# An attention and gated-MLP kernel on one core: fewer zero-weight matmuls, ten exponential buffers, other constants in the planner

## The chip, the cores and the metric

The kernel runs on one core of a Trainium2 chip. The metric is the device time of one execution in microseconds. The kernel before took 746.0 us (median of three runs, 745.09 to 746.49). The profile shown here is of one more execution, which took 744.99 us, with a span of 743.1 us from its first to its last instruction.

Five engines work side by side, each on its own queue of instructions: TensorE (PE: matmuls; PEld: its weight loads), VectorE (DVE), ScalarE (ACT), GpSimd (POOL) and SyncE (SP, here only DMA issues). They wait for one another by semaphores.

## The reference

```python
xn = layernorm(x)                          # x: 1 x 2048 x 512
q = (xn @ wq) as 32 heads of 16; k = xn @ wk; v = xn @ wv     # one k and v for all heads
p = softmax(q @ k.T * 16**-0.5)            # 2048 x 2048 for each of 32 heads
s = (p @ v, heads side by side) @ wo
h = silu(xn @ w_gate) * (xn @ w_up)        # 512 -> 1792
g = silu(h @ w_down)
out = x + s * g
```

The bulk is the exponential of 32 x 2048 x 2048 scores.

## The kernel before

Scores are made transposed, 128 keys by 512 queries of one head in a matmul that uses 32 rows of the array. Two heads fill one *score tile* of 128 x 1024 in PSUM (`sc_emit`, L890). There are 1024 score tiles, in 32 blocks (4 query chunks x 4 groups of 8 heads x 2 halves), 32 tiles to a block. Three PSUM rings of 1024 columns hold them: rings 0 and 1 serve ScalarE, ring 2 serves VectorE.

The exponential of a tile is taken on one of two engines:

- ScalarE: one `ACTIVATE Exp` from ring 0 or 1 into a bf16 buffer `Pb` (`act_sc`, L950). The first few of block 1 go into the space of `g2_sb` instead (8 tiles).
- VectorE: a bit trick in two passes. `passA` (L1004) turns a tile of ring 2 into integers whose bits read as fp16; two tiles make a *pair*, and two shifted copies (`dS`, L1020) are added, so that three approximations with different errors are summed by the matmuls.

The products with V (`pv_emit`, L760) accumulate in the one bank `o_ps`. They use 32 columns of the array for each head, so four matmuls (a *column group*) run side by side. A pair of ScalarE tiles costs one column group with `VA`, a VectorE pair three with `VD`. At the end of a block VectorE moves `o_ps` out (`oev`, L773). Between these TensorE also does the MLP, the Q projections and the output projection as *fill* column groups into `m_ps` (`cmm`, L491); ScalarE does 72 `Tanh` for the two silus, 56 for the gate (L666) and 16 after the down projection (L686).

All of this is interleaved by a planner that runs while the program is built. `_Sched` gives each operation an engine, a planned duration and its dependencies, and places it at the earliest planned time; `pe_pick` chooses what TensorE does next. Then everything is emitted in planned order, and each engine's queue is chained in that order. Planned times therefore decide only the order; on the chip the semaphores decide when.

Names that the change touches:

- `MMF` is the planned duration of a column group or of a score tile, `SWITCH` the planned cost of going from score matmuls (row strips) to column groups or back.
- `TOL`: a column group may go ahead of the next ScalarE score tile if it ends at most `TOL` after the time at which that tile could start.
- `NPB` is the number of `Pb` buffers. The exponential of tile k writes buffer k mod `NPB`, and waits for the column group that read the tile `NPB` earlier (`pb_rel`).
- `PB_URG`: as long as fewer than that many ScalarE tiles are outstanding (their column group is not yet placed), column groups of the current block rank behind fill; from there on they rank first.
- `ACTMIN`: where nothing is ready for TensorE for at least one column group and a switch, `pe_pick` puts a group of four matmuls with zero weights there (`zw`), which adds nothing to the open sum in `o_ps` or `m_ps`. It does so only if `activity`, the planned TensorE work that started in the last 1.8 us (a score tile counts 0.107 us, transposes and the small V projections nothing), is under `ACTMIN`. With 9.0 that is always so.

The lines that decide it:

```python
if Tz - F >= MMF + sd.switch("c") and (act_ < ACTMIN or cur["issued"] == NTILE):
    ...
            return F, ("zero", bb)
...
ex = OP("ACT", 0.904, [sc, pb_rel[k - NPB] if k >= NPB else None, cur["exp"]], emit, (1,), name="exp")
...
if ts is None or tm + sd.switch(co.mode) + co.dur <= ts + TOL:
    cands.append(tm)
```

Of the kernel before, what the change touches and what calls it, by code (L numbers as in the profile page):

```python
# [32 lines left out]
NWARM, NJUNK = 13, 200  # L33
D_START, D_LIM, D_LIM_END = 26, 12, 8
F_ON, F_OFF = 26, 60
PB_URG, AHEAD, LAZY, ACTMIN, ACTLOW = 6, 16, 8, 9.0, 0.8
DPRI, DTOL, DWIN = -1.0, 0.12, 0.15
TOL, MERGE = 0.17, 0.25


def _dims(A_x, A_wq, B_w_gate):
# [143 lines left out]
class _Sched:  # L185
    LAT = {"PE": 0.205, "ACT": 0.22, "DVE": 0.25, "POOL": 0.16, "DMA": 0.0, "EXT": 0.0}
    SAME = {"PE": 0.0, "ACT": 0.0, "DVE": 0.1, "POOL": 0.05, "DMA": 0.0}
    SWITCH = 0.105
    HOT = 0.3
    LOCKS = ("dS", "xn")  # L190

# [40 lines left out]
    def switch(self, mode):  # L232
        return self.SWITCH if self.mode is not None and mode != self.mode else 0.0

# [51 lines left out]
def kernel(  # L286
# [13 lines left out]
    nc = tc.nc  # L300
# [72 lines left out]
    xn = [sb([P, D], BF16, f"xn{i}") for i in range(4)]  # L373
    res = xn
    QB = [sb([P, 512], BF16, f"QB{i}") for i in range(2)]
    NPB = 8
    Pb = [sb([P, 1024], BF16, f"Pb{i}") for i in range(NPB)]
    XB = [g2_sb[:, 2 * i:2 * i + 2, :].rearrange("p n d -> p (n d)") for i in range(NT // 2)]
    Bf = [sb([P, 2048], U16, f"Bf{i}")[:] for i in range(6)]
# [117 lines left out]
    def OP(eng, dur, deps, emit, prio, mode=None, name=""):  # L497
        return sd.new(_Op(eng, dur, deps, emit, prio, mode, name))
# [3 lines left out]
        o.start = o.end = t  # L502
        return o

    MMF = 0.215
    NBLK = NSC * NQ * 2
    LN = 4 * (NSC - 1)
    NTILE = NBLK * NT * 2
# [144 lines left out]
    def hT_use(sc, f):  # L653
        return [hT_rd[0][1]] if hT_rd[0] is not None and hT_rd[0][0] == sc - 1 else []
    hT_last = [None]

    def g_ffn(sc, f):
# [3 lines left out]
        def mm(w, kc):  # L661
# [3 lines left out]
        s_ = OP("DVE", 0.6, [a, ab_rel[i]], lambda: nc.vector.tensor_copy(out=ab[i][:], in_=m_ps[:]), (1,), name="gev")  # L665
# [4 lines left out]
        u_ = OP("DVE", 0.6, [t_, b], lambda: nc.vector.scalar_tensor_tensor(  # L670
            out=th[i][:], in0=th[i][:], scalar=1.0, in1=m_ps[:], op0=ALU.add, op1=ALU.mult), (1,), name="umul")
        m_rel[:] = [u_]
        h = OP("POOL", 1.25, [u_, s_] + hT_use(sc, f), lambda: nc.gpsimd.tensor_tensor(  # L673
            out=hT[:, f, :], in0=ab[i][:], in1=th[i][:], op=ALU.mult), (0,), name="hmul")
        ab_rel[i] = th_rel[i] = h
        h_done[f] = h
# [256 lines left out]
    def act_sc(i, b, x, start, dur=MMF):  # L933
# [7 lines left out]
        else:  # L941
            cur["ba"] = b
            k = cur["nA"]
            cur["nA"] += 1
            buf = Pb[k % NPB][:]
            pb_rel.append(None)
        if k >= NPB:
            assert pb_rel[k - NPB] is not None
        def emit():
            bi = nc.scalar.activation(out=buf, in_=ring[i][:], func=ACT.Exp, scale=escale, bias=ebias)  # L950
            if k >= NPB:
                tc.declare_no_dep(bi.ins, exp_ins[k - NPB].ins,
# [457 lines left out]
```

## Time and profile before

| | |
|---|---|
| median of three runs | 746.0 us |
| the profiled execution | 744.99 us, span 743.1 us |
| mean granted TensorE clock | 0.996 |
| busy: TensorE, ScalarE, VectorE, GpSimd | 721.5, 718.1, 682.4, 127.0 us |
| ScalarE exponentials | 736, of 1181 ns each (728 into `Pb`, 8 of 1148 ns into `g2_sb`) |
| score tiles on VectorE | 288 (144 pairs), `passA` 1219 ns |

Busy time of a group of instructions is the union of their intervals. Consecutive ScalarE instructions overlap in the trace (one starts before the other has ended), so the step from start to start, not the duration, is what one costs. The ends of matmuls are modelled. "Idle before" is the time in which an engine had nothing in flight, with what ended it. A DMA is not the limit anywhere after the first 40 us: the mean over the span is 28 GB/s.

### The profile page before, as it was taken

What the parts mean: (1) busy time and instruction counts of PE and PEld (TensorE: products, weight loads), DVE (VectorE), ACT (ScalarE), POOL (GpSimd) and SP (SyncE); (2) the same over time, 40 slices, a digit from 0 to 9 for tenths busy, and PEclk for the clock granted to TensorE, in tenths of its full rate; (3) what the DMA queues carried; (4) which work ended last, traced back from release to release, by engine and by line L of the source; (5) the groups of instructions that cost most, each with busy time, mean ns of one, the idle gap of its engine ahead of it and who ended that gap; (6) DMA issues with size and microseconds to landing.
All of it is one profiled execution on the core that took longest, in us unless ns stands there. A gap on an engine that the chain in (4) does not pass through costs nothing.

```text
span 743.1 us, 20569 instructions
## 1 busy us (share of the span) xinstructions
PE 721.5 (97%) x8999; PEld 217.0 (29%) x8999; DVE 682.4 (92%) x886; ACT 718.1 (97%) x822; POOL 127.0 (17%) x120
## 2 busy tenths in 40 slices
PE   8999999999999999999999999999999999999994
PEld 3332222222222222222222322222222322322231
DVE  7779999999999899999999999999989999999995
ACT  5999999999999999999999999999999999999992
POOL 3212222200022222200013121220003222220001
PEclk9999999999999999999999999999999999999998
DMA  9400000000011100000001000000001000000001
GB/s 326 151 24 3 23 3 23 2 11 17 3 30 38 38 3 8 18 2 24 3 25 45 21 19 3 25 2 9 17 2 31 24 23 3 6 20 2 24 30 34
DMA packets 21722, 20.68 MB, mean 28 GB/s; under 512 B 8760, under 2 KB 17720, under 8 KB 21624
## 3 DMA queue, kind: packets, MB, share of 16 engines
q1 hardware_dynamic: 20040, 18.73, 8.3%
q8 instruction: 72, 1.18, 0.7%
q10 hardware_dynamic: 1584, 0.56, 0.3%
q14 instruction: 26, 0.21, 0.1%
HBM read 14.71 MB, written 2.34 MB: 23 GB/s over the span
## 4 chain that ended last, share of the span: by engine, by line
ACT 59%; PE 34%; DVE 4%; issue 2%; POOL 0%; ACTq 0%; DVEq 0%; POOLq 0%
ACT Pb L950 54%; PE ring L890 12%; PE o_ps L760 12%; PE m_ps L491 9%; ACT th L666 3%; ACT g_sb L950 1%; DVE Bf L1020 1%; DVE Bf L1004 1%; ACT th L686 1%; DVE x_sb L1020 1%; DVE x_sb L1004 1%; PE ring L491 0%; DVE ab L665 0%; PE ring L455 0%; DVE xn L708 0%
## 5 line engine op out<-in xcount | busy, mean ns | idle before, releaser
L950 ACT ACTIVATE Pb<-ring 128x1024 bf16<-128x1024 f32 x728 | 687.9, 1181 | 3.8 <-PE ring L890 1.9
L890 PE MATMUL ring<-QB,KT 32*128 32x512 bf16 x2048 | 291.7, 383 | 7.1 <-ACT Pb L950 3.9
L1004 DVE TENSOR_SCALAR Bf<-ring 128x1024 uint16<-128x1024 f32 x172 | 209.7, 1219 | 10.9 <-PE ring L890 9.2
L890 PEld LDWEIGHTS <-KT 32*128 32x128 bf16 x2048 | 84.9, 91 | 301.2 <-issue 297.1
L1004 DVE TENSOR_SCALAR x_sb<-ring 128x1024 uint16<-128x1024 f32 x116 | 141.5, 1220 | 7.6 <-PE ring L890 5.8
L760 PE MATMUL o_ps<-Pb,VA 128*32 128x512 bf16 x1456 | 140.5, 385 | 0.0
L673 POOL TENSOR_TENSOR hT<-ab,th 128x512 bf16<-128x512 f32 x56 | 78.2, 1396 | 356.7 <-DVE th L670 356.7
L760 PE MATMUL o_ps<-Bf,VD 128*32 128x512 f16 x1044 | 95.1, 384 | 1.2 <-DVE Bf L1020 1.1
L491 PE MATMUL m_ps<-wd_sb,hT 128*32 128x512 bf16 x896 | 72.5, 382 | 0.0
L491 PE MATMUL m_ps<-xnT,wg_sb 128*32 128x512 bf16 x896 | 72.3, 383 | 0.1
L1020 DVE TENSOR_SCALAR Bf<-Bf 128x2048 uint16<-128x2048 uint16 x101 | 72.1, 723 | 0.2
L491 PE MATMUL m_ps<-xnT,wu_sb 128*32 128x512 bf16 x896 | 68.4, 382 | 0.0
L760 PE MATMUL o_ps<-x_sb,VD 128*32 128x512 f16 x684 | 64.1, 384 | 0.0
L760 PEld LDWEIGHTS <-VD 128*32 128x32 f16 x1728 | 38.4, 94 | 60.1 <-issue 50.5
L760 PEld LDWEIGHTS <-VA 128*32 128x32 bf16 x1472 | 36.8, 94 | 54.2 <-issue 50.6
L1020 DVE TENSOR_SCALAR Bf<-x_sb 128x2048 uint16<-128x2048 uint16 x74 | 50.8, 694 | 0.3
L1020 DVE TENSOR_SCALAR x_sb<-Bf 128x2048 uint16<-128x2048 uint16 x71 | 50.5, 716 | 0.4
L745 POOL TENSOR_TENSOR oT<-oa,rb 128x512 bf16<-128x512 f32 x15 | 19.7, 1313 | 162.8 <-DMA rb<-dscr 153.0
L665 DVE COPY ab<-m_ps 128x512 f32<-128x512 f32 x56 | 38.3, 685 | 6.8 <-PE m_ps L491 6.4
L666 ACT ACTIVATE th<-ab 128x512 f32<-128x512 f32 x56 | 43.7, 781 | 0.0
L670 DVE SCALAR_TENSOR_TENSOR th<-th,m_ps 128x512 f32<-128x512 f32 x56 | 38.2, 682 | 4.0 <-PE m_ps L491 3.4
L1020 DVE TENSOR_SCALAR x_sb<-x_sb 128x2048 uint16<-128x2048 uint16 x42 | 29.5, 703 | 0.1
(115 smaller groups left out, 332.8 us busy)
## 6 DMA issues: line engine op xcount, KB each, us to landing
rb<-dscr SPq DMA_DIRECT2D x15, 256.0 KB
out_dram<-xn SPq DMA_DIRECT2D x16, 128.0 KB, 1.9
dn<-oa SPq DMA_DIRECT2D x120, 2.0 KB, 1.7
oa<-oa SPq DMA_DIRECT2D x60, 32.0 KB, 2.0
wg_sb<-in_B_w_gate_dram SPq DMA_DIRECT2D x1, 1792.0 KB, 11.6
wu_sb<-in_B_w_up_dram SPq DMA_DIRECT2D x1, 1792.0 KB
wd_sb<-in_B_w_down_dram SPq DMA_DIRECT2D x1, 1792.0 KB, 20.5
x_sb<-in_A_x_dram SPq DMA_DIRECT2D x3, 512.0 KB
```

Of the source, the lines that this page charges most:

```text
L491: return [nc.tensor.matmul(out=dst[GRP * j:GRP * j + GRP, :], lhsT=w[:, GRP * j:GRP * j + GRP], rhs=rhs, start=start, stop=stop, tile_posi ...
L665: s_ = OP("DVE", 0.6, [a, ab_rel[i]], lambda: nc.vector.tensor_copy(out=ab[i][:], in_=m_ps[:]), (1,), name="gev")
L666: t_ = OP("ACT", 0.477, [s_, th_rel[i]], lambda: nc.scalar.activation(out=th[i][:], in_=ab[i][:], func=ACT.Tanh, scale=0.5), (0,), name="t ...
L670: u_ = OP("DVE", 0.6, [t_, b], lambda: nc.vector.scalar_tensor_tensor(out=th[i][:], in0=th[i][:], scalar=1.0, in1=m_ps[:], op0=ALU.add, op ...
L673: h = OP("POOL", 1.25, [u_, s_] + hT_use(sc, f), lambda: nc.gpsimd.tensor_tensor(out=hT[:, f, :], in0=ab[i][:], in1=th[i][:], op=ALU.mult) ...
L686: t_ = OP("ACT", 0.477, [a, th_rel[i]], lambda: nc.scalar.activation(out=th[i][:, :D], in_=m_ps[:, :D], func=ACT.Tanh, scale=0.25), (0,), ...
L745: return [pk, q], lambda eng: eng.tensor_tensor(out=oT[qs % 2][:, jj, :], in0=o0[:], in1=rbt[:], op=ALU.mult)
L760: r.append(nc.tensor.matmul(out=o_ps[GRP * g:GRP * g + GRP, :], lhsT=lhs, rhs=rhs, start=(n == 0), stop=(n == pv_total[(b, g)] - 1), tile_ ...
L890: return lambda: [nc.tensor.matmul(out=ring[sl][:, u * 512:(u + 1) * 512], lhsT=KT[half][GRP * g:GRP * g + GRP, t * P:(t + 1) * P], rhs=QB ...
L950: bi = nc.scalar.activation(out=buf, in_=ring[i][:], func=ACT.Exp, scale=escale, bias=ebias)
L1004: lambda: nc.vector.tensor_scalar(out=U[:, hs], in0=ring[si][:], scalar1=ubias, scalar2=UINF, op0=ALU.add, op1=ALU.min), (1.5, u), name="p ...
L1020: o = OP("DVE", 0.6, [pa, pa0] + wrel, lambda wi=wi, i=i: nc.vector.tensor_scalar(out=Bf[wi], in0=U, scalar1=SHIFT[i], scalar2=None, op0=A ...
```

## The change

Nothing in the kernel's arithmetic changes, only constants: those of the planner, the count of `Pb` buffers, and the planned duration of one GpSimd operation.

```diff
-PB_URG, AHEAD, LAZY, ACTMIN, ACTLOW = 6, 16, 8, 9.0, 0.8
+PB_URG, AHEAD, LAZY, ACTMIN, ACTLOW = 9, 16, 8, 0.6, 0.8
-TOL, MERGE = 0.17, 0.25
+TOL, MERGE = 0.21, 0.25
-    SWITCH = 0.105
+    SWITCH = 0.11
-    NPB = 8
+    NPB = 10
-    MMF = 0.215
+    MMF = 0.216
-        h = OP("POOL", 1.25, [u_, s_] + hT_use(sc, f), lambda: nc.gpsimd.tensor_tensor(
+        h = OP("POOL", 1.3, [u_, s_] + hT_use(sc, f), lambda: nc.gpsimd.tensor_tensor(
```

Counted over the whole program, the order of instructions changes as follows.

| | before | now |
|---|---|---|
| zero-weight column groups into `o_ps` / into ring 2 | 84 / 1 | 17 / 0 |
| ScalarE exponentials | 736 | 738 |
| VectorE tiles (`passA`) | 288 | 286 |
| column groups with `VA` / `VD` | 368 / 432 | 369 / 429 |
| fill column groups | 808 | 808 |
| steps from one ScalarE score tile to the next with no or one column group between (fill and zero groups count, transposes and V projections do not) | 63 | 94 |
| the same with two | 477 | 466 |
| the same with three or more | 195 | 177 |

TensorE early in the program, around the fourth and fifth ScalarE score tile (`ring0`, `ring1`; `zw` are the zero weights, `KT` the keys, `VA` the values). Before (each row stands for its two or four strips, weight loads left out):

```order
L890 MATMUL ring1_97<-QB0_118,KT0_84 128x512
L760 MATMUL o_ps_99<-Pb0_120,VA_86 32x512
L760 MATMUL o_ps_99<-Pb1_121,VA_86 32x512
L760 MATMUL o_ps_99<-xnT_81,zw_149 32x512
L890 MATMUL ring0_96<-QB0_118,KT0_84 128x512
```

Now, the same place and a little on:

```order
L890 MATMUL ring1_97<-QB0_118,KT0_84 128x512
L760 MATMUL o_ps_99<-Pb0_120,VA_86 32x512
L760 MATMUL o_ps_99<-Pb1_121,VA_86 32x512
L890 MATMUL ring0_96<-QB0_118,KT0_84 128x512
L1259 MATMUL ring2_98<-x_sb_101,ident_bf_61 128x512
```

The zero group after the column group is gone, and the next score tile follows directly; behind it one plain matmul with the identity stands where before two zero groups stood.

TensorE at the last of the four V projections (L472, 16 small matmuls), before. The rows lie between the 32nd and the 33rd ScalarE score tile:

```order
L890 MATMUL ring1_97<-QB0_118,KT0_84 128x512
L491 MATMUL m_ps_100<-xnT_81,hT_107 32x512
L472 MATMUL ring2_98<-wv_sb_103,xnT_81 128x16
L760 MATMUL o_ps_99<-Pb4_124,VA_86 32x512
L760 MATMUL o_ps_99<-Pb6_126,VA_86 32x512
L890 MATMUL ring0_96<-QB0_118,KT0_84 128x512
```

Now, between the 30th and the 32nd:

```order
L890 MATMUL ring1_97<-QB0_118,KT0_84 128x512
L472 MATMUL ring2_98<-wv_sb_103,xnT_81 128x16
L890 MATMUL ring0_96<-QB0_118,KT0_84 128x512
L760 MATMUL o_ps_99<-Pb6_126,VA_86 32x512
L760 MATMUL o_ps_99<-Pb8_128,VA_86 32x512
L890 MATMUL ring1_97<-QB0_118,KT0_84 128x512
```

Before, two fill groups, the projection and two column groups with `VA` stood between two score tiles; now the projection stands alone, and the two column groups come after the next score tile.

TensorE around the 521st ScalarE score tile, before. Its exponential writes `Pb0`, and the column group that reads `Pb0`'s older content (with `Pb1`'s) is the last row:

```order
L890 MATMUL ring0_96<-QB1_119,KT0_84 128x512
L760 MATMUL o_ps_99<-Bf4_132,VD_109 32x512
L760 MATMUL o_ps_99<-x_sb_101,VD_109 32x512
L890 MATMUL ring1_97<-QB1_119,KT0_84 128x512
L890 MATMUL ring2_98<-QB1_119,KT0_84 128x512
L760 MATMUL o_ps_99<-Pb1_121,VA_86 32x512
L760 MATMUL o_ps_99<-Pb0_120,VA_86 32x512
```

Now the one place where a reader of a `Pb` buffer still stands behind the score tile whose exponential overwrites it is the 729th (the second row from below; its exponential writes `Pb0`):

```order
L890 MATMUL ring1_97<-QB1_119,KT1_85 128x512
L890 MATMUL ring2_98<-QB1_119,KT1_85 128x512
L760 MATMUL o_ps_99<-Bf1_131,VD_109 32x512
L760 MATMUL o_ps_99<-Bf0_130,VD_109 32x512
L890 MATMUL ring0_96<-QB1_119,KT1_85 128x512
L760 MATMUL o_ps_99<-Pb0_120,VA_86 32x512
```

Before, the reader stands two column groups and two score tiles behind (the 521st and the 681st tile alike; the 49th has it one score tile and its VectorE tile behind); now it stands directly behind.

## Rows read from the trace of the kernel before

**Rows 1.** The page, part 1: busy us, share of span, instructions.
```profile
PE 721.5 (97%) x8999; PEld 217.0 (29%) x8999; DVE 682.4 (92%) x886; ACT 718.1 (97%) x822; POOL 127.0 (17%) x120
```

**Rows 2.** Busy us by engine (PE, PEld, DVE, ACT, POOL); clock, DMA share, GB/s.
```profile
100.00:150.00 50.00, 49.25 (x616) 14.83 (x616) 47.48 (x60) 50.00 (x59) 10.95 (x8) 1.00 0.04 10
```

**Rows 3.** ScalarE in order of time: start, length, merged instructions.
```profile
300.37 6.61 ACT L950 ACTIVATE Pb<-ring 128x1024 bf16<-128x1024 f32 x7
306.70 0.78 ACT L666 ACTIVATE th<-ab 128x512 f32<-128x512 f32 x1
307.22 5.76 ACT L950 ACTIVATE Pb<-ring 128x1024 bf16<-128x1024 f32 x6
```

**Rows 4.** Line 950: count, least, median, longest ns, first and last start.
```profile
L950 ACT ACTIVATE Pb<-ring x728: 1006/1187/1355, 12.9 to 727.3; 128x1024 bf16<-128x1024 f32 x182
```

**Rows 5.** TensorE in order of time, an ordinary stretch.
```profile
303.68 0.40 PE L760 MATMUL o_ps<-Bf,VD 128*32 128x512 f16 x4
303.90 0.60 PE L491 MATMUL m_ps<-xnT,wg_sb 128*32 128x512 bf16 x8
304.44 0.39 PE L890 MATMUL ring<-QB,KT 32*128 32x512 bf16 x2
304.76 0.61 PE L491 MATMUL m_ps<-xnT,wg_sb 128*32 128x512 bf16 x8
305.31 0.40 PE L890 MATMUL ring<-QB,KT 32*128 32x512 bf16 x4
```

**Rows 6.** All zero-weight matmuls, by line: count, busy us, mean ns.
```profile
L760 PE MATMUL o_ps<-xnT,zw 128*32 128x512 bf16 x336 | 27.6, 383 | 0.0
```

**Rows 7.** ScalarE in order of time, around its three longest waits.
```profile
38.43 3.88 ACT L950 ACTIVATE Pb<-ring 128x1024 bf16<-128x1024 f32 x4
43.12 2.85 ACT L950 ACTIVATE Pb<-ring 128x1024 bf16<-128x1024 f32 x3 [0.81 <-PE ring L890]
...
507.58 10.36 ACT L950 ACTIVATE Pb<-ring 128x1024 bf16<-128x1024 f32 x11
518.83 1.94 ACT L950 ACTIVATE Pb<-ring 128x1024 bf16<-128x1024 f32 x2 [0.89 <-PE o_ps L760]
...
675.07 1.94 ACT L950 ACTIVATE Pb<-ring 128x1024 bf16<-128x1024 f32 x2 [0.89 <-PE o_ps L760]
```

**Rows 8.** TensorE in order of time, the same waits.
```profile
40.56 0.39 PE L890 MATMUL ring<-QB,KT 32*128 32x512 bf16 x2
...
41.43 0.56 PE L472 MATMUL ring<-wv_sb,xnT 128*128 128x16 bf16 x16
41.91 0.84 PE L760 MATMUL o_ps<-Pb,VA 128*32 128x512 bf16 x8
42.69 0.61 PE L890 MATMUL ring<-QB,KT 32*128 32x512 bf16 x6
...
518.38 0.83 PE L760 MATMUL o_ps<-Pb,VA 128*32 128x512 bf16 x12
```

**Rows 9.** Waits, all engines: us in total, times, longest.
```profile
DVE Bf L1004 <- PE ring L890: 9.2, 26, 0.8
...
PE o_ps L760 <- DVE Bf L1020: 1.1, 4, 0.4
```

**Rows 10.** The end: VectorE's last move of `o_ps`, TensorE's next weight load.
```profile
728.95 0.76 DVE L773 COPY oa<-o_ps 128x256 f32<-128x256 f32 x2 [1.54 <-PE o_ps L760]
...
729.92 0.20 PEld L1050 LDWEIGHTS ring<-ident_f,oa 128*128 128x128 f32 x2 [0.42 <-DVE oa L773]
```

**Rows 11.** Stretches at the end; columns as in Rows 2 (PEclk: granted clock).
```profile
734.00:736.00 2.00, 0.00 (x0) 0.00 (x0) 1.97 (x5) 0.00 (x0) 1.96 (x2) 1.00 0.21 68
736.00:738.00 2.00, 0.00 (x0) 0.00 (x0) 0.88 (x1) 0.00 (x0) 0.33 (x1) 0.70 0.41 124
```

**Rows 12.** One early stretch, instructions on `zw` alone: PE, PEld, DVE, clock.
```profile
23.00:26.00 3.00, 0.00 (x0) 0.00 (x0) 0.00 (x0) 1.00 1.08 340
```

**Rows 13.** The same stretch, instructions on `xn` alone (PE: transposes).
```profile
23.00:26.00 3.00, 0.74 (x8) 0.53 (x8) 1.11 (x4) 0.00 (x0) 1.00 1.08 340
```

## Prediction

> **What bounds the kernel now.** I began with the busy times. Two engines share the top: TensorE with 721.5 us and ScalarE with 718.1 us of a span of 743.1 us, both 97% [rows 1]. The reader is to see that the two figures do not mean the same. In the stretch from 100 to 150 us ScalarE has an instruction in flight for all of the 50 us [rows 2], so the next look is whether it really runs without a pause. In the order of time, seven exponentials start at 300.37 and the next instruction starts at 306.70: 6.33 / 7 = 0.904 us for each, though each lasts about 1.19 us [rows 3, 4]. A `Tanh` takes from 306.70 to 307.22, 0.52 us. So ScalarE's floor is a sum of steps: 735 steps of 0.904 us between the first and the last exponential (736 of them, 728 on line 950 into `Pb` and 8 into `g2_sb`), 664.4 us, and 72 `Tanh` at 0.52 us, 37.4 us; 701.8 us together. The first starts at 12.9 and the last at 727.3 [rows 4]: 714.4 us. ScalarE is late by 714.4 - 701.8 = 12.6 us in all, and short waits hide behind the overlap: six exponentials from 307.22 to 312.70 take 5.48 us where 5.42 would do [rows 3].
>
> So ScalarE is the bound, and what can be won is at most these 12.6 us, plus what a smaller number of exponentials would save. TensorE's 97% holds zero-weight matmuls for 27.6 us [rows 6], so it is not full of work; but it is in order, and what stands in front of a score tile can make ScalarE wait. From the trace, a score tile to the first column group takes 304.44 to 304.76 = 0.32 us, the next column group 0.22 us (303.68 to 303.90), two groups and the way back 0.55 us (304.76 to 305.31) [rows 5]. With two column groups between, a step takes 0.87 us, under 0.904; with three it takes 1.09 us, and ScalarE's lead shrinks by 0.18 us.
>
> **The change part by part.**
>
> *Exponentials.* There are two more on ScalarE (738): 2 x 0.904 = +1.81 us, all of it on the path, since ScalarE is the bound. VectorE has two tiles less. That is off the path: VectorE waited 9.2 us for score tiles at line 1004 alone [rows 9].
>
> *Ten buffers and `PB_URG` 9.* Before, the exponential of tiles 521 and 681 waits for a column group that stands behind two other column groups and two further score tiles on TensorE. The eleven exponentials from 507.58 last 10.36 us, so the last starts at 507.58 + 10.36 - 1.19 = 516.75 and the next could start at 517.65; it starts at 518.83, after the column groups that began at 518.38 [rows 7, 8]. That is 1.18 us. The wait at 675.07 shows the same 0.89 us of visible idle time, so I price it alike: 2 x 1.18 = -2.36 us. Now the order has one such place, tile 729, with the reader directly behind the tile. Its cost is 0 if ScalarE has its usual lead; otherwise the step to a column group, 0.32 us; at worst a whole wait as above, 1.18 us. I take the 0.32, since the distance is the shortest possible. Sum -2.04 us. Behind a waiting exponential stand all later exponentials and `Tanh`, and behind them the rings; nothing else can fill ScalarE.
>
> *The V projection.* At 43.12 ScalarE starts after four exponentials that began at 38.43 and lasted 3.88 us: due at 38.43 + 3.88 - 1.19 + 0.90 = 42.02, it was 1.10 us late [rows 7]. TensorE shows why: from the score tile at 40.56 to the one at 42.69 there are 2.13 us, with two fill groups, the 16 small matmuls (41.43 to 41.91, 0.48 us) and two column groups [rows 8]. Now only the 16 matmuls stand there: 0.32 + 0.48 + 0.33 for the way back = 1.13 us, 0.23 us over a step. Gain 1.10 - 0.23 = -0.87 us. If other transposes crowd that place it is 0; at best 1.10.
>
> *The zero groups themselves.* 67 of 84 are gone, and one into ring 2: 68 x 0.22 = 15 us of TensorE. By the plan each stood in a gap; on the chip only those cost something whose gap was not there. What this, `TOL`, `MMF` and `SWITCH` do together I read from the order: steps with three or more column groups fall from 195 to 177. 72 of them are paid for by a `Tanh` (0.52 us more room), which leaves 123 and 105. Of the 12.6 us the three long waits are 2.36 + 1.10, so 9.1 us are short ones, 9.1 / 123 = 0.074 us for each crowded step. 18 fewer: -1.3 us. The bounds: all of the short waits go (-9.1), or the wider `TOL` (0.04 us more) and `SWITCH` (0.005) are paid in full in each of the 105 steps (+4.7). I take -1.3 because the count of crowded steps is what the order shows; the 0.045 us is a permission, and whether it is used is not seen.
>
> *VectorE's shifts.* Four column groups waited for line 1020, 1.1 us of TensorE in all [rows 9]. The planned VectorE times have not changed, so I leave this at 0, with -1.1 to +1.1.
>
> *GpSimd's 1.25 to 1.3 and the end.* The operation itself is the same, and GpSimd is busy for 127 us of 743 [rows 1]: 0. In the last stretch the first transpose of the last block waits for VectorE's move of `o_ps` (728.95 + 0.76 = 729.71, weight load at 729.92 [rows 10]), not for the fill groups before it, of which there are two fewer now: 0, at best -0.4.
>
> Sum: 1.81 - 2.04 - 0.87 - 1.3 = -2.4 us. The profiled execution took 744.99 us (1.9 us around its span of 743.1) and would take 742.6. It lies 1.0 us under the median of the runs, 746.0; from the median the forecast is 743.6 us.
>
> **The clock.** The zero groups also keep TensorE's array at work, and taking them out could cost the clock. In the trace the granted clock is 1.00 (2.4 GHz) until the matmuls end at about 734; it is still 1.00 in 734 to 736, with no matmul, and falls to 0.70 on average in 736 to 738 [rows 11]. From 23 to 26 us, without one zero matmul and with eight transposes among the score tiles, it stayed 1.00 [rows 12, 13].
> The Trainium skill says otherwise of transposes (TensorE: Matmul & The Clock Gate, "Part 4: PE-mode transpose"): a transpose does not count as work for the clock the way other matmuls do. By that rule the early stretch, where transposes now stand with fewer zero groups around them, is the one that could slow. The trace of before does not contradict it, since score tiles and V projections stood between the transposes; no stretch here holds transposes alone.
>
> **The rivals.**
>
> *TensorE is the bound.* Its 97% speaks for it, its zero matmuls against. If its 15 us of removed groups came off, ScalarE's floor would stop it: all 12.6 us of lateness gone, 1.81 added, about 746.0 - 10.8 = 735; a half of it 740.
>
> *Nothing to see.* The two more exponentials and the new wait at tile 729 eat the gain, and the short waits stay: 1.81 - 2.36 + 1.18 - 0.87 = -0.2, so 745.8. For it: the removed zero groups stood in planned gaps. Against it: the two long waits have no place left in the order.
>
> *Slower: the wider tolerance.* Place: the crowded steps. `TOL` lets a third column group go ahead although the score tile could start 0.21 us earlier. If half of the 0.045 us is paid in all 177 steps, 4 us, and the -1.3 does not come: 1.81 - 2.04 - 0.87 + 4 = +2.9, so 749. It decides from 1.1 us on (1.81 - 2.04 - 0.87 = -1.1), which is 0.006 us for each of the 177 steps. Against it: 94 steps now have no or one column group (63 before), and each of those gives the lead back.
>
> *Slower: the clock falls early.* Place: score tiles 4 to 31. At 1.2 GHz a step with two groups takes 1.74 instead of 0.87 us, with three 2.2 us, 0.84 and 1.3 us over a step of ScalarE. There are about seven such steps: +6 us, 749.6. Against it: [rows 12].
>
> **How the numbers follow.** A difference under 0.2% (1.5 us) cannot be told from none. The forecast, a gain of 1.5 to 5 us, 741 to 744.5, has 0.50. TensorE as the bound, 735 to 741, has 0.08. Nothing to see, 744.5 to 747.5, has 0.27. The tolerance, 747.5 to 751, has 0.10; the clock 0.05. Faster: 0.50 + 0.08 = 0.58; same 0.27; slower 0.15. The likeliest case's own range is 741 to 744.5; eight times in ten needs the case of no change and half of the last steps on either side: 739 to 747.5.
>
> **What would show it.** Right: no exponential waits 0.9 us for `o_ps` at the ends of blocks; ScalarE steps of 0.904 us still dominate; last start minus first start near 712 us, with 737 steps and 72 `Tanh` as its floor (703.7), so lateness near 8.5 us; one wait of some 0.3 us near tile 729; at the V projection a wait of 0.2 us instead of 1.1; the granted clock at 1.00 up to the end of the matmuls. Wrong: lateness above 11 us, from many steps of 0.93 to 1.0 us (tolerance); a clock under 1.00 between 15 and 45 us; or TensorE waiting at line 760 for line 1020 more than 2 us, which would mean that VectorE's planned times, which I left alone, now decide.

## The result and the profile after

The changed kernel takes 750.77 us (median of eight runs, 748.2 to 764.18) against 745.73 us before (eight runs, 745.09 to 746.6): a ratio of 1.0063, interval 1.0045 to 1.0081. It is slower, outside the predicted range. The profiled execution took 752.13 us, with a span of 750.3 us and a mean granted clock of 0.979 (0.996 before); over all eight runs it lies between 0.955 and 0.991. Runs that lie more than 1.5% above the fastest of their kernel, as the 764.18 here, are left out of every ratio and kept in the medians, and the profiles of f1 and e6 below are of such runs.

The first look is at the page of the changed kernel: busy times, and the granted clock in 40 slices of 18.8 us each.

```profile
PE 716.2 (95%) x8720; PEld 213.9 (29%) x8720; DVE 677.1 (90%) x882; ACT 721.6 (96%) x824; POOL 127.0 (17%) x120
...
PEclk9999999999999999999999999999999999999757
...
L950 ACT ACTIVATE Pb<-ring 128x1024 bf16<-128x1024 f32 x730 | 691.6, 1172 | 6.7 <-PE ring L890 5.0
```

TensorE is busy for 5.3 us less than before [rows 1], and the kernel is longer all the same. The row that differs is the clock's: 7 and 5 tenths in two of the last three slices.

I then took ScalarE's floor apart as in the prediction, at 0.904 us after an exponential, 0.52 after a `Tanh` of the gate and 0.477 after one of the 16 others; lateness is what the steps take beyond that (13.2 us before by this count, where the prediction took 0.52 for all `Tanh` and had 12.6).

| profiled execution, us | before | after | difference |
|---|---|---|---|
| first exponential starts | 12.87 | 13.87 | +1.00 |
| floor (736 and 738 exponentials) | 701.2 | 703.0 | +1.81 |
| lateness before 700 us | 12.87 | 11.63 | -1.24 |
| lateness after 700 us | 0.35 | 6.80 | +6.45 |
| last exponential's start to the end | 15.83 | 15.05 | -0.78 |
| span | 743.1 | 750.3 | +7.2 |

The loss lies after 700 us, in the last 32 exponentials. ScalarE there, in order of time:

```profile
698.67 11.43 ACT L950 ACTIVATE Pb<-ring 128x1024 bf16<-128x1024 f32 x12
710.32 4.85 ACT L950 ACTIVATE Pb<-ring 128x1024 bf16<-128x1024 f32 x5 [0.22 <-PE ring L890]
...
719.12 1.02 ACT L950 ACTIVATE Pb<-ring 128x1024 bf16<-128x1024 f32 x1 [0.47 <-PE ring L890]
720.63 1.02 ACT L950 ACTIVATE Pb<-ring 128x1024 bf16<-128x1024 f32 x1 [0.49 <-PE ring L890]
722.14 1.02 ACT L950 ACTIVATE Pb<-ring 128x1024 bf16<-128x1024 f32 x1 [0.49 <-PE ring L890]
...
725.72 1.02 ACT L950 ACTIVATE Pb<-ring 128x1024 bf16<-128x1024 f32 x1 [1.04 <-PE o_ps L760]
```

From 719.12 on, a step takes 1.51 us (720.63 - 719.12) instead of 0.904, and each of them waits for a score tile. What TensorE did before, in order of time:

```profile
702.92 0.40 PE L760 MATMUL o_ps<-Pb,VA 128*32 128x512 bf16 x4
703.50 0.40 PE L890 MATMUL ring<-QB,KT 32*128 32x512 bf16 x4 [0.17 <-ACT Pb L950]
704.41 0.39 PE L890 MATMUL ring<-QB,KT 32*128 32x512 bf16 x2 [0.52 <-ACT Pb L950]
704.73 0.62 PE L760 MATMUL o_ps<-Pb,VA 128*32 128x512 bf16 x4
705.33 0.61 PE L890 MATMUL ring<-QB,KT 32*128 32x512 bf16 x4
```

The same column group takes 0.40 us at 702.92 and 0.62 at 704.73. Nothing late stood before it: TensorE waited 0.17 and 0.52 us for ScalarE to free a ring. The stretches of the changed kernel (columns as in [rows 2]):

```profile
695.00:700.00 5.00, 5.00 (x68) 1.27 (x60) 4.90 (x8) 5.00 (x7) 0.00 (x0) 1.00 0.16 32
702.00:704.00 2.00, 1.51 (x18) 0.58 (x15) 1.96 (x4) 2.00 (x3) 0.51 (x1) 1.00 0.19 64
704.00:706.00 2.00, 1.59 (x14) 0.47 (x13) 1.79 (x2) 2.00 (x4) 1.04 (x1) 0.68 0.00 0
706.00:708.00 2.00, 2.00 (x14) 0.34 (x11) 1.82 (x2) 2.00 (x3) 0.00 (x0) 0.50 0.00 0
720.00:724.00 4.00, 4.00 (x36) 0.70 (x32) 2.13 (x3) 2.53 (x4) 0.00 (x0) 0.50 0.02 4
728.00:732.00 4.00, 4.00 (x52) 0.92 (x44) 3.12 (x5) 3.22 (x5) 0.00 (x0) 0.92 0.00 0
```

and of the kernel before, at the same time:

```profile
704.00:708.00 4.00, 4.00 (x50) 1.19 (x48) 3.52 (x5) 4.00 (x6) 0.00 (x0) 1.00 0.02 6
```

The clock falls from 1.00 (2.4 GHz) to 0.50 (1.2 GHz) at about 704.7 us and is back at full at 728.6. Before the fall TensorE was busy for 1.51 of 2 us, never idle longer than 0.52; before the change it was busy throughout at this time. Idle time of that size does not tell a fall by itself. The kernel before has two such waits in a row at about 315 us, and its clock stays at 1.00:

```profile
314.45 0.39 PE L890 MATMUL ring<-QB,KT 32*128 32x512 bf16 x2 [0.32 <-ACT Pb L950]
315.37 0.40 PE L890 MATMUL ring<-QB,KT 32*128 32x512 bf16 x4 [0.53 <-ACT Pb L950]
```

Which part of the sparse work decides is not read from these rows. In the trace of the changed kernel the MLP's fill ends at 686.4 us, some 45 ScalarE tiles before the end (718.6 us and 10 tiles before the change), and from 700.8 to 717 us 15 of the 17 steps from one ScalarE score tile to the next hold one column group or none. Zero groups would have filled them, but the planner counts too much activity to put them there (e3 below allows them, and 31 stand in the last 50 tiles).

### The profile page after: what moved, and what is told of

Same layout as the page of the kernel before. It is cut to its first block, busy times and chain, and to the rows that moved or that the text cites. A ratio compares the mean times of both kernels' runs of the same rounds, so it can differ in the third digit from the quotient of the medians.

```text
span 750.3 us, 20016 instructions
## 1 busy us (share of the span) xinstructions
PE 716.2 (95%) x8720; PEld 213.9 (29%) x8720; DVE 677.1 (90%) x882; ACT 721.6 (96%) x824; POOL 127.0 (17%) x120
## 4 chain that ended last, share of the span: by engine, by line
ACT 55%; PE 35%; DVE 5%; issue 2%; DMA 1%; POOL 1%; SPq 0%; DVEq 0%; POOLq 0%; ACTq 0%
ACT Pb L950 51%; PE ring L890 12%; PE o_ps L760 11%; PE m_ps L491 10%; ACT th L666 3%; DVE Bf L1004 1%; ACT g_sb L950 1%; DVE Bf L1020 1%; DVE x_sb L1004 1%; ACT th L686 1%; DMA rb<-dscr 1%; DMA dscr<-rc 0%; DMA dn<-oa 0%; SPq L787 0%; DVE x_sb L1020 0%
## 5 line engine op out<-in xcount | busy, mean ns | idle before, releaser
L890 PE MATMUL ring<-QB,KT 32*128 32x512 bf16 x2048 | 297.1, 388 | 16.4 <-ACT Pb L950 13.6
L1004 DVE TENSOR_SCALAR Bf<-ring 128x1024 uint16<-128x1024 f32 x176 | 214.7, 1220 | 14.5 <-PE ring L890 12.9
L1004 DVE TENSOR_SCALAR x_sb<-ring 128x1024 uint16<-128x1024 f32 x110 | 134.1, 1219 | 7.3 <-PE ring L890 5.4
L760 PE MATMUL o_ps<-Pb,VA 128*32 128x512 bf16 x1460 | 136.4, 389 | 0.0
L491 PE MATMUL m_ps<-xnT,wu_sb 128*32 128x512 bf16 x896 | 70.5, 383 | 0.1
L1020 DVE TENSOR_SCALAR Bf<-Bf 128x2048 uint16<-128x2048 uint16 x98 | 67.5, 696 | 0.3
L760 PEld LDWEIGHTS <-VD 128*32 128x32 f16 x1716 | 40.5, 95 | 56.2 <-issue 44.6
L1020 DVE TENSOR_SCALAR x_sb<-Bf 128x2048 uint16<-128x2048 uint16 x78 | 54.8, 708 | 0.3
L773 DVE COPY oa<-o_ps 128x512 f32<-128x512 f32 (+1 forms) x33 | 22.1, 672 | 8.6 <-PE o_ps L760 8.2
## 6 DMA issues: line engine op xcount, KB each, us to landing
wg_sb<-in_B_w_gate_dram SPq DMA_DIRECT2D x1, 1792.0 KB, 11.4
```

Source lines behind the costliest of these rows:

```text
L491: return [nc.tensor.matmul(out=dst[GRP * j:GRP * j + GRP, :], lhsT=w[:, GRP * j:GRP * j + GRP], rhs=rhs, start=start, stop=stop, tile_posi ...
L760: r.append(nc.tensor.matmul(out=o_ps[GRP * g:GRP * g + GRP, :], lhsT=lhs, rhs=rhs, start=(n == 0), stop=(n == pv_total[(b, g)] - 1), tile_ ...
L773: oev[b] = sd.new(_Op("DVE", 0.6, [], lambda: [nc.vector.tensor_copy(out=oat[:, a:z], in_=o_ps[:, a:z]) for a, z in cuts], (0.2,), name="o ...
L890: return lambda: [nc.tensor.matmul(out=ring[sl][:, u * 512:(u + 1) * 512], lhsT=KT[half][GRP * g:GRP * g + GRP, t * P:(t + 1) * P], rhs=QB ...
L1004: lambda: nc.vector.tensor_scalar(out=U[:, hs], in0=ring[si][:], scalar1=ubias, scalar2=UINF, op0=ALU.add, op1=ALU.min), (1.5, u), name="p ...
L1020: o = OP("DVE", 0.6, [pa, pa0] + wrel, lambda wi=wi, i=i: nc.vector.tensor_scalar(out=Bf[wi], in0=U, scalar1=SHIFT[i], scalar2=None, op0=A ...
```

## The experiments

Theory A, formed from these rows: the clock's fall at the end costs most of the loss, and it needs two edits together, one that ends the fill early and one that takes the zero groups out of the hole. Theory B: the sparse order itself costs the time, and the clock only shows it. Lateness below is read from one profiled execution each, as in the table above; "line 734" is VectorE's idle time before the reciprocal of the denominators, in us. The times are medians. Each ratio is to runs of the kernel before on the same chip, whose medians were 745.68 to 746.21.

| kernel | tiles on ScalarE, zero groups | us, ratio to before (interval) | lateness to 700 us, after | line 734 |
|---|---|---|---|---|
| before | 736, 85 | 745.73 | 12.9, 0.4 | 1.8 |
| after | 738, 17 | 750.77, 1.0063 (1.0045 to 1.0081) | 11.6, 6.8 | 3.2 |
| e1 | 736, 75 | 747.68, 1.0023 (1.0014 to 1.0032) | 15.9, 0.9 | 4.1 |
| e2 | 738, 11 | 748.9, 1.0041 (1.0026 to 1.0056) | 15.6, 0.7 | 4.5 |
| e3 | 740, 42 | 748.24, 1.0041 (1.0028 to 1.0054) | 12.5, 1.4 | 2.8 |
| e8 | 740, 100 | 748.25, 1.0033 (1.002 to 1.0046) | 13.3, 1.5 | 3.4 |
| f1 | 738, some 32 | 746.53, 1.0005 (0.9995 to 1.0015) | 24.5, 0.8 | 2.9 |
| f2 | 740, 72 | 752.2, 1.0088 (1.0075 to 1.0101) | 11.4, 4.9 | 2.6 |
| e6 | 738, 11 | 754.52, 1.0074 (1.0055 to 1.0093) | 26.0, 0.7 | 2.1 |
| h2 | 736, 63 | 756.09, 1.0129 (1.0113 to 1.0145) | 23.9, 1.3 | 2.7 |
| g3 | 736, 85 | 745.22, 0.9992 (0.9983 to 1.0001) | 12.9, 0.8 | 1.8 |
| e7 | 734, 10 | 743.67, 0.9968 (0.9956 to 0.998) | 15.3, 0.4 | 3.7 |
| g1 | 734, 57 | 748.98, 1.0049 (1.0036 to 1.0061) | 17.0, 1.3 | 7.2 |
| g2 | 738, 65 | 753.39, 1.0096 (1.0081 to 1.0112) | 21.2, 0.8 | 9.3 |
| h1 | 734, 62 | 748.59, 1.0035 (1.0022 to 1.0047) | 18.7, 0.6 | 7.8 |
| i1 | 732, 54 | 741.13, 0.9936 (0.9922 to 0.9949) | 12.0, 0.4 | 0.3 |
| i2 | 740, 10 | 744.99, 0.9991 (0.9982 to 1.0) | 10.0, 0.3 | 0.9 |
| i5 | 736, 85 | 746.43, 1.0004 (0.9995 to 1.0013) | 13.1, 1.6 | 0.2 |

### Which edit makes the clock fall

**e1**: the changed kernel with the zero groups back.

```diff
-PB_URG, AHEAD, LAZY, ACTMIN, ACTLOW = 9, 16, 8, 0.6, 0.8
+PB_URG, AHEAD, LAZY, ACTMIN, ACTLOW = 9, 16, 8, 9.0, 0.8
```

> The changed kernel with ACTMIN back at 9.0, all else of the change kept; 75 zero groups, 28 of them in the last 50 ScalarE tiles; 736 exponentials. Theory A (the clock falls in the sparse last blocks because the zero groups are missing there): the granted clock stays at 1.00 to the end of the matmuls, mean 0.995, the 6.8 us of lateness after 700 us are gone, time 743 to 745.5, faster than before or equal. Theory B (the order of the last blocks itself, few column groups and much VectorE work, costs the time, and the clock falls only as a result): lateness after 700 us stays at 5 us or more, time 749 to 751. Theory C (the wider tolerance costs a little everywhere): time 747 to 750, lateness spread over the span.

747.68 us. The clock stays up and the lateness after 700 us goes to 0.9, but the kernel is not as fast as Theory A had it: 15.9 us of lateness lie before 700. The time is in the range of Theory C, but the changed kernel has the same `TOL` and 11.6 us of lateness before 700, less than the kernel before (12.9), so the wider tolerance alone does not explain it. What does stays open.

**e2**: the kernel before, with the zero groups taken out (`ACTMIN` 9.0 to 0.6).

> The kernel before with ACTMIN 0.6 alone: 11 zero groups, all in the first 40 tiles; fill lasts to the end of the last block as before (two to three column groups a step in the last 50 tiles); 738 exponentials. Theory A: the clock stays at 1.00, mean 0.995, since the last blocks are full; time 746 to 748, by the two more exponentials (+1.8 us) less at most a microsecond for zero groups that were in the way. Rival (zero groups are needed anywhere in the program): clock 0.98 or less, 749 to 752.

748.9 us, a miss as well. Its fill lasts to the end, and the clock does not fall there in the profiled execution (0.7 us late after 700), so `ACTMIN` alone does not make the fall at the end. Three of its seven executions have a mean clock of 0.991 or 0.992; where theirs fell is not known.

**e3**: the changed kernel with zero groups for the last 100 tiles alone.

```diff
-        if Tz - F >= MMF + sd.switch("c") and (act_ < ACTMIN or cur["issued"] == NTILE):
+        if Tz - F >= MMF + sd.switch("c") and (act_ < (ACTMIN if cur["issued"] < NTILE - 100 else 9.0) or cur["issued"] == NTILE):
```

> The changed kernel with ACTMIN 0.6 up to 100 tiles before the end and 9.0 from there: 42 zero groups, 31 of them in the last 50 ScalarE tiles, 10 in the first 40; 740 exponentials. Theory A: the clock stays at 1.00 to the end of the matmuls, time 744 to 747 (two more exponentials than in the changed kernel cost 1.8 us of the 6.8 us won). If zero groups were needed early or in the middle: clock under 1.00 before 700 us, 748 to 751.

**e8**: the kernel before with ten buffers and `PB_URG` 9 alone.

> The kernel before with ten buffers and PB_URG 9 alone: 100 zero groups, 29 in the last 50 ScalarE tiles; 740 exponentials; the fill runs out some 20 tiles before the end as in the changed kernel. Theory A: the zero groups hold the clock at 1.00; the two waits of 1.18 us for a buffer go, four more exponentials cost 3.6 us, so 745 to 748. Theory B (the sparse order itself costs the time): lateness of 5 us or more after 700 us, 750 to 753.

Both keep the clock (0.996 and 0.995). In e8 the fill ends early too (at 693.4 us), and 29 zero groups stand in the last 50 tiles. So `PB_URG` and the buffers together make the hole (either by itself was not tried) and `ACTMIN` leaves it open; neither part alone brings the fall at the end. Both kernels take 748.2 us, more than Theory A had, with 740 exponentials on ScalarE, four more than before (3.6 us). Every one of these edits also draws a new order with another count of tiles; the next two kernels therefore keep the order.

**f1**: the changed kernel's own order, with some 15 zero groups written into the planned gaps of the last 80 tiles when it is emitted.

```diff
...
+if o.eng == "PE" and o.start > tail0:
+    for _ in range(int((o.start - pe_end + 0.08) / 0.33)):
+        ...   # four matmuls of zw into the open sum in o_ps
```

> The changed kernel in exactly its own order, with some 15 zero groups put into the open sum of the last blocks where the plan leaves a gap of a group's length; nothing else moves. Theory A (the 6.8 us of lateness after 700 us come from the halved clock): the clock stays at 1.00 to the end of the matmuls, mean 0.995, lateness after 700 us at most 1.5 us, time 744 to 746.5. Theory B (the order of the last blocks costs the time, the clock only follows): time 749 to 752, lateness after 700 us 5 us or more.

**f2**: the order of e8, with the 28 zero groups of the last blocks left out when it is emitted.

> The kernel with ten buffers and PB_URG 9 alone (748.25 us), in exactly its own order, with the 28 zero groups of the last blocks left out; nothing else moves. Theory A: with the zero groups gone the clock falls to 0.5 somewhere after 695 us, mean 0.985 or less, lateness after 700 us 5 to 9 us, time 752 to 757. Theory B: the clock stays, 747.5 to 748.5.

f1 takes 746.53 us, 4.2 under the changed kernel; f2 takes 752.2, 4.0 over e8. The mean granted clocks of the executions that the ratios use go with it: 0.978 to 0.991 in the changed kernel and 0.990 to 0.996 in f1, 0.995 or 0.996 in e8 and 0.980 to 0.987 in f2. Stretches of f1:

```profile
700.00:704.00 4.00, 2.94 (x34) 0.93 (x30) 3.88 (x6) 4.00 (x6) 0.00 (x0) 1.00 0.07 23
720.00:724.00 4.00, 3.78 (x48) 1.22 (x44) 3.81 (x5) 4.00 (x6) 0.00 (x0) 1.00 0.00 0
```

and of f2:

```profile
708.00:712.00 4.00, 3.56 (x26) 0.75 (x24) 3.40 (x6) 4.00 (x5) 0.00 (x0) 0.69 0.00 0
```

TensorE of f1 is busy for only 2.94 of 4 us at 700 and keeps its clock: again the busy share of one stretch does not tell a fall. ScalarE at the end of f1, in order of time:

```profile
699.88 37.01 ACT L950 ACTIVATE Pb<-ring 128x1024 bf16<-128x1024 f32 x40
```

Forty exponentials without a pause: 37.01 us, where 39 x 0.904 + 1.18 is 36.4. And of f2, from which only zero groups were taken:

```profile
719.78 1.02 ACT L950 ACTIVATE Pb<-ring 128x1024 bf16<-128x1024 f32 x1 [0.92 <-PE ring L890]
721.29 1.02 ACT L950 ACTIVATE Pb<-ring 128x1024 bf16<-128x1024 f32 x1 [0.49 <-PE ring L890]
724.22 11.11 ACT L950 ACTIVATE Pb<-ring 128x1024 bf16<-128x1024 f32 x12 [1.90 <-PE o_ps L760]
```

with the 1.51 us step of the changed kernel again (721.29 - 719.78). Added work makes it faster and removed work slower, in one and the same order: Theory B falls. The clock's fall at the end costs about 4 us (4.2 and 4.0 by the medians). With the clock held, the changed order is as fast as the kernel before (ratio 1.0005) and no faster.

The 24.5 us of lateness that f1 has before 700 us come from another fall, in its profiled execution, from 18.3 to 55.9 us:

```profile
25.00:50.00 25.00, 24.76 (x186) 7.67 (x184) 10.24 (x24) 17.60 (x18) 3.32 (x9) 0.50 0.13 38
```

f1 has the changed kernel's order there, so the changed kernel can fall early too. Its run of 764.18 us, with a mean clock of 0.955, may be such a case; it has no trace.

**e6**: the changed kernel with eight buffers and `PB_URG` 6.

> The changed kernel with NPB 8 and PB_URG 6 as before, all else of the change kept, ACTMIN 0.6 too: 11 zero groups, none after the first 40 tiles; fill reaches the last block, two or more column groups a step in the last 20 us; 738 exponentials. Theory A (ACTMIN does harm only together with the buffers, which use the fill up early): clock 0.995, 746 to 749, with waits for a buffer of 1 us or so back. Rival (ACTMIN alone slows the end): clock 0.985 or less, 750 to 753.

754.52 us, outside both ranges. Its seven executions fall in three groups by mean granted clock: 750.23 to 751.14 us at 0.996, 754.52 and 754.66 at 0.987, and 764.19 and 765.21 at 0.969 and 0.968. Only the one of 764.19 has a trace. There the clock is 0.50 from 18.3 to 59.3 us and 1.00 at the end, as Theory A wants. But even at the mean clock of the kernel before this order takes 4 to 5 us more than it. Of those, 1.8 us are two exponentials; the rest stays open.

**h2**: the kernel before, its order kept, with the 22 zero groups of the first 40 tiles left out.

> The kernel before in exactly its own order, with the 22 zero groups of the first 40 ScalarE tiles left out; the other 63 stay. If the missing early zero groups are what let the clock fall at 18 us in some executions of the kernels with ACTMIN 0.6: the clock falls to 0.5 between 15 and 30 us in most executions, 752 to 762, mean clock 0.96 to 0.98, and stays at 1.00 at the end. If the early stretch has work enough: 745 to 747, clock 0.995.

756.09 us. Stretches of h2:

```profile
14.00:15.00 1.00, 0.39 (x2) 0.09 (x2) 0.97 (x4) 1.00 (x3) 0.49 (x2) 1.00 1.04 409
16.00:17.00 1.00, 0.47 (x4) 0.10 (x3) 0.96 (x4) 1.00 (x2) 0.74 (x1) 1.00 1.03 409
18.00:19.00 1.00, 1.00 (x10) 0.77 (x8) 1.00 (x4) 1.00 (x2) 0.00 (x0) 0.54 1.03 405
20.00:25.00 5.00, 4.37 (x32) 1.50 (x33) 4.14 (x12) 4.14 (x5) 1.01 (x1) 0.50 1.10 349
55.00:60.00 5.00, 4.74 (x58) 1.44 (x54) 4.19 (x5) 4.34 (x6) 0.00 (x0) 0.94 0.00 0
```

and of the kernel before:

```profile
14.00:15.00 1.00, 1.00 (x12) 0.30 (x11) 0.96 (x5) 1.00 (x2) 0.59 (x2) 1.00 1.04 409
```

Without its early zero groups TensorE is busy for 0.39 and 0.47 of 1 us at 14 and 16, the clock falls at 18.1, and it comes back only at 55.6: meanwhile ScalarE falls behind (25.2 us of lateness in all against 13.2, and the medians differ by 10).

### What the buffers are worth

**g3**: the order of the kernel before, planned for eight buffers, with ten in memory.

```diff
-    NPB = 8
+    NPB, NREAL = 8, 10
...
-            buf = Pb[k % NPB][:]
+            buf = Pb[k % NREAL][:]
...
```

> The kernel before in exactly its own order, with ten physical buffers for eight, the planner still planning for eight. The two waits of 1.18 us for a buffer (tiles 521 and 681) cannot arise. If they are lost time: -2.4 us, 743.2 to 744, lateness of ScalarE 10.5 to 11 us for 13.2. Rival (the time is lost again at the next wait, since TensorE is as far behind): 745 to 746.

745.22 us, ratio 0.9992: no difference that can be told. The two waits of [rows 7] are gone at their places, but not the time. ScalarE of g3 in order of time:

```profile
507.64 12.19 ACT L950 ACTIVATE Pb<-ring 128x1024 bf16<-128x1024 f32 x13
...
676.93 2.98 ACT L950 ACTIVATE Pb<-ring 128x1024 bf16<-128x1024 f32 x3 [0.67 <-PE ring L890]
```

The second wait comes back 1.9 us later as one for a score tile: TensorE was behind, and the buffer only showed it first. By the starts of the single exponentials g3 gains 1.16 us on the kernel before at tile 521 and has 0.18 of it left at tile 528; it gains 1.16 at tile 681 and has 0.22 left at tile 683.

### Filling the end otherwise, and a second cause

**e7**: the changed kernel with its fill spread to the end of the program. The planner spreads the fill from `F_ON` score tiles after the start to `F_OFF` before the end.

```diff
-F_ON, F_OFF = 26, 60
+F_ON, F_OFF = 26, 10
```

> The changed kernel with F_OFF 10 for 60: the MLP's fill is spread to the last blocks, two to three column groups a step there; ACTMIN stays at 0.6, 10 zero groups in all, none in the last 600 tiles; 734 exponentials. Theory A: useful work holds the clock as well as zeros, clock 0.995, lateness after 700 us at most 1.5 us; four exponentials fewer than changed (-3.6 us) and 6 us less lateness: 742 to 746. If zero groups themselves were needed: clock 0.985 or less, 748 or more.

743.67 us, faster than both kernels. Lateness after 700 us is 0.4, without a zero group there. Two exponentials fewer than before are 1.8 of the 2.3 us by which it is under the 745.96 of its own chip's runs of before. The clock still fell once in the profiled execution, and the mean clocks of the six lie between 0.991 and 0.997. Stretches of e7:

```profile
490.00:492.00 2.00, 1.31 (x12) 0.36 (x12) 2.00 (x3) 2.00 (x4) 1.37 (x1) 1.00 0.00 0
492.00:493.00 1.00, 0.61 (x2) 0.20 (x2) 1.00 (x2) 1.00 (x3) 0.00 (x0) 0.51 0.00 0
496.00:500.00 4.00, 4.00 (x40) 0.88 (x36) 2.79 (x4) 2.64 (x4) 0.00 (x0) 0.65 0.01 1
```

So I tried zero groups there too, in three ways. **g1**: e7's order with 47 zero groups in planned gaps everywhere. **g2**: the changed kernel's order with 48, likewise. **h1**: e7 with `ACTMIN` 1.2.

> The kernel with the fill spread to the end (F_OFF 10, 743.67 us) in exactly its own order, with 47 zero groups put into the open sum wherever the plan leaves a gap of a group's length, among them those around the 490th ScalarE tile, where its clock fell at 492 us and ScalarE lost some 3 us. Theory A: clock 1.00 to the end of the matmuls, mean 0.995 or more, the 3 us at 495 to 500 us gone: 740.5 to 743. Rival (groups in planned gaps cost as much as they hold): 743.5 to 746.

> The changed kernel in exactly its own order, with 48 zero groups put into the open sum wherever the plan leaves a gap of a group's length, early ones too (tiles 4 to 9). Theory A (all that the change lost is the clock, at the end in every run and early in some): no execution over 749 us, clock 0.995, 744.5 to 746.5, so equal to before; the order by itself wins nothing, as the runs with the clock held at the end have shown so far (746.5). If the order by itself wins the 2.4 us of the prediction: 742.5 to 744.

> The changed kernel with F_OFF 10 and ACTMIN 1.2: the fill lasts to the end, and the planner itself puts 62 zero groups where the array has worked little (22 of them in the first 40 tiles); 734 exponentials. If the two faults of the change are the clock at the end and the too small threshold: clock 0.995, no fall in the middle, 741.5 to 744, faster than before and at least equal to the kernel with F_OFF 10 alone (743.67). Rival (zero groups that the planner places cost as much as they hold): 744 to 747.

Each lies outside both of its ranges: 748.98, 753.39 and 748.59 us. The last column of the table names what they share: VectorE stands still before line 734 for 7.2 to 9.3 us. VectorE in h1, in order of time:

```profile
517.92 0.68 DVE L1020 TENSOR_SCALAR x_sb<-x_sb 128x2048 uint16<-128x2048 uint16 x1
520.50 0.35 DVE L734 RECIPROCAL rc<-dn 128x32 f32<-128x32 f32 x1 [1.89 <-DMA dn<-oa]
520.77 1.16 DVE L1004 TENSOR_SCALAR Bf<-ring 128x1024 uint16<-128x1024 f32 x1
```

The reciprocal stands at its place in VectorE's queue and its denominators have not landed; behind it wait `passA`, behind that TensorE's column group, behind that the next score tile. TensorE and ScalarE of h1:

```profile
521.98 0.58 PE L760 MATMUL o_ps<-Bf,VD 128*32 128x512 f16 x2 [1.34 <-DVE Bf L1004]
```
```profile
523.58 1.02 ACT L950 ACTIVATE Pb<-ring 128x1024 bf16<-128x1024 f32 x1 [2.04 <-PE ring L890]
```

and the clock of h1:

```profile
518.00:522.00 4.00, 2.66 (x38) 0.65 (x31) 2.11 (x5) 3.53 (x4) 0.00 (x0) 1.00 0.13 26
522.00:523.00 1.00, 1.00 (x10) 0.17 (x9) 1.00 (x2) 0.00 (x0) 0.00 (x0) 0.53 0.27 49
```

The idle TensorE loses its clock as well. Each of the five waits of 0.9 us or more at line 734 of h1 is followed within 4 us by a step of ScalarE that is 0.5 to 2.2 us late. g2 shows the same at 524.74 (a wait of 1.89 us, and the clock at 0.50 from 528 to 530). So a DMA does limit after the first 40 us, by the time at which it lands and not by its rate. To test this alone, the last three kernels change one number, the planned time of that DMA, which puts the reciprocal later in VectorE's order:

```diff
-        dens_op[b] = OP("DMA", 2.4, [ev], dens, (0,))
+        dens_op[b] = OP("DMA", 4.0, [ev], dens, (0,))
```

**i1** is h1 with it:

> The changed kernel with F_OFF 10, ACTMIN 1.2 and a planned time of 4.0 instead of 2.4 for the denominators' DMA, so that the reciprocal stands later in VectorE's order; 732 exponentials on ScalarE, 54 zero groups (22 in the first 40 tiles). If the waits of line 734 for its DMA are the second cause: they fall from 7.8 us to about 2 us, ScalarE is late by some 12 us instead of 19, and with two exponentials fewer (1.8 us) the kernel takes 741 to 744 us. If they only show a lateness that has another cause: the waits go, the lateness stays near 18 us elsewhere, and it takes 745.5 to 748 us.

**i2** is e7 with it:

> The changed kernel with F_OFF 10 and a planned time of 4.0 instead of 2.4 for the denominators' DMA, ACTMIN 0.6 as in the change; 740 exponentials on ScalarE, against 734 without the second edit (743.7 us, line 734 waits 3.7 us). If the waits are a cause: six more exponentials, +5.4 us, and some 2 to 3 us of lateness less, 745.5 to 747.5 us. If they are not: 748.5 to 750 us.

**i5** is the kernel before with it:

> The kernel before with a planned time of 4.0 instead of 2.4 for the denominators' DMA and nothing else; 736 exponentials on ScalarE as before. Line 734 waits only 1.6 us for its DMA there, so if these waits are a cause at most 1 us can go: 744.5 to 746.5 us, no difference that can be told. If the later place of the reciprocal has a price of its own (o_ps or rc free later), 747 us or more.

i1 and i5 came out as the first theory had it, i2 a little below even that. i1 takes 741.13 us, 7.5 less than h1 and the fastest of all; line 734 in i1, with all that it waited for:

```profile
L734 DVE RECIPROCAL rc<-dn x15: 337/344/354, 76.0 to 692.5; 128x32 f32<-128x32 f32 x15
...
  DMA dn<-oa: 0.3, 1
```

Its lateness is 12.4 us in all, where h1 has 19.3; the other 1.8 us are two exponentials. i2 has six exponentials more than e7 (5.4 us) and takes 1.3 us more, with 10.3 us of lateness for 15.6. Of these 5.3 us, 3.1 are four late steps of e7 right after its clock fell at 492 us, a fall that i2's profile does not have, so 2.2 us at most are left for the waits. i5, where only 1.6 us of waits for that DMA could go, shows no difference. In none of the three profiles does the clock fall before 730 us. The orders of i1 and i2 differ from h1 and e7 in more than the reciprocal, so the reciprocal's part in their gain is bounded, not isolated; that the lateness fell with it in two orders, and not where there was nothing to win, speaks for it. For g1 and g2 this cause is read from their waits alone: neither was run with the later reciprocal.

## Why the prediction was wrong, by its own steps

**The clock** is the step that failed. The rival was there, with 0.05 and +6 us, but at score tiles 4 to 31 alone, and "the granted clock at 1.00 up to the end of the matmuls" stood in the list of what would show me right. I had counted steps with three column groups over the whole program (195 and 177), and the steps with one or none (63 and 94) I wrote down as a reason against being slower, since each gives the lead back. Of those 31 more sparse steps about 14 stand among the last 50 steps, where the fill has run out (19 there by the trace, 5 before), and these were the loss. An order of the last 50 tiles, before and now, would have shown them. That the price came near (+6.45 us of lateness in the profiled execution, about 4 us by f1 and f2, against +6) is luck, since I had worked it out for other steps, and a step with two groups took 1.51 us at half clock where I had 1.74. The early place was real too: h2 shows about +10 us there, more than my +6, for I counted seven steps at half clock, and the low clock lasted from 18 to about 55 us. The changed kernel keeps some early zero groups (the first at 15.3 us), and its profiled execution has a clock of 1.00 there.

My evidence against it, [rows 12], was read wrongly: a stretch without zero groups at full clock shows that this stretch was full of other work (TensorE is busy for 2.82 of its 3 us), not that zero groups can be spared elsewhere. The rule on transposes (the Trainium skill, TensorE: Matmul & The Clock Gate, "Part 4: PE-mode transpose") did not decide it: from 702 to 706 us TensorE ran score tiles and column groups alone, and the clock fell there. In h2 it did so too from 14.1 us to the fall at 18.1, and the next transposes begin at 18.13. No run here has a stretch of transposes alone.

**Ten buffers and `PB_URG` 9.** Forecast -2.04. No exponential of the profile after waits for `o_ps` before the clock falls, so the waits went as I had it; but g3, with nothing else changed, gains 0.8 us by its medians and none that can be told. A wait that ends last is worth only the distance to the next one. The changed kernel shows it as well: tile 522 starts 0.91 us late at 520.78, for a score tile, after line 734 has waited 0.99 us at 517.40. `PB_URG` 9 was priced at nothing beyond that, and together with the buffers it makes the fill run out early. The wait near tile 729 came (1.04 us at 725.72), in the low clock, where its size says nothing of the 0.32.

**The zero groups themselves and the short waits.** Forecast -1.3, measured about 0: up to 700 us, steps that are late by under 0.3 us sum to 8.3 us before and 8.4 after. That fits "by the plan each stood in a gap": taking them out gave nothing.

**The V projection.** Forecast -0.87, measured -1.07 at that place: no exponential is late there any more. The projection stands between the score tiles at 39.97 and 40.78, a step of 0.81 us where I had 1.13, since I had added a way back of 0.33 that the 0.48 already held. A new wait of 0.41 us stands shortly before, at 37.80, behind transposes that waited for VectorE; my proviso that other transposes may crowd the place comes near it. Together that is -0.66. TensorE after:

```profile
36.83 0.61 PE L455 MATMUL ring<-ident_bf,xn 128*128 128x128 bf16 x8 [0.42 <-DVE xnT L461]
...
40.29 0.56 PE L472 MATMUL ring<-wv_sb,xnT 128*128 128x16 bf16 x16
```

**VectorE's shifts.** Left at 0 with bounds of 1.1; TensorE now waits 2.4 us for line 1020, 2.0 of them for `Bf` (1.1 before [rows 9]), so this sign of being wrong came, if barely. The longest goes with a late ScalarE. After, VectorE, TensorE and ScalarE in order of time:

```profile
259.02 1.75 DVE L1020 TENSOR_SCALAR Bf<-x_sb 128x2048 uint16<-128x2048 uint16 x1
260.70 0.68 DVE L665 COPY ab<-m_ps 128x512 f32<-128x512 f32 x1
```
```profile
260.83 0.40 PE L760 MATMUL o_ps<-Bf,VD 128*32 128x512 f16 x4 [0.91 <-DVE Bf L1020]
```
```profile
261.41 0.63 ACT L666 ACTIVATE th<-ab 128x512 f32<-128x512 f32 x1 [0.55 <-DVE ab L665]
```

The shift takes 1.75 us for its usual 0.68, while GpSimd runs line 673 beside it; that this is the cause is not shown. ScalarE's `Tanh` is 0.79 us late at 261.41, not through TensorE but through VectorE's own queue: it waits for the copy of line 665, which stands behind the long shift.

**Exponentials**: +1.81 in the floor, as forecast. **The end**: 0.78 us shorter against 0 to -0.4; that stretch takes 14.4 to 16.1 us over nearly all kernels here (20.1 in e6), so I read no cause into it. The first exponential's start, +1.0, is of this execution (12.9 to 13.1 in the profiles of the other kernels) and is not the change's.

So of -2.4 us the exponentials and the V projection held in the main, the buffers and short waits (-3.3) did not come, and the fall of the clock came from a place I had not looked at: 6.45 us in the profiled execution, about 4 by the medians. Without it, in f1, the changed order takes 746.53 us, which is my rival "nothing to see" and not my forecast. So the gain would not have come with the clock held either.

## What to carry to other kernels

Filler work in an engine that is not the bound is not free to take out: look at what is left in each stretch after it, the last one above all, and not at counts over the program. A removed wait is worth the distance to the next late thing, so keep the order fixed and change one resource before you price it. Where a planner sets the order, one constant redraws everything: compare orders with the same work in them, or subtract what differs (here 0.904 us for each exponential moved to ScalarE) before a cause is named.

## What the runs showed that I had not expected

- TensorE's clock fell with the engine never idle for more than 0.52 us and busy for 1.51 of the 2 us before; and it stayed low for some 24 us, though the engine was then busy throughout (4.00 of 4 us at 720). In h2 it stayed low for some 37 us. Yet f1 kept its clock with TensorE busy for 2.94 of 4 us at 700, so these runs do not show what idle time brings the fall.
- One order can keep or lose some of its clock from one execution to the next: e6 took 750.2 us at a mean clock of 0.996, 754.5 at 0.987 and 765.2 at 0.968.
- One number for a DMA's duration in the planner, 2.4 or 4.0 us, went with 7.5 us of kernel time (h1 and i1). In h1 VectorE's queue stands still at the reciprocal while its data is under way.
